# Four edits to the plan of a fused HGRN2 and multiplicative-FFN kernel on one Trainium2 core

## The chip, the core and the metric

The kernel runs on one core of one Trainium2 chip. The metric is device time in microseconds (us), the median of several executions. A profile of one further execution shows every instruction of the engines: TensorE (PE, with its weight loads as PEld), VectorE (DVE), ScalarE (ACT), GpSimd (POOL) and SyncE (SP), which issues the DMAs.

## What is computed

Two stages follow each other. The first is a gated linear recurrence for 4 batches of 8 heads, 768 steps and head size 48; the second is a feed-forward block on the 3072 resulting rows of 384.

```python
f = 1.0 / (1.0 + np.exp(-f_logit))
for t in range(S):
    state = f[:, :, t, :, None] * state + np.einsum('bhd,bhe->bhde', k[:, :, t], v[:, :, t])
    y[:, :, t] = np.einsum('bhd,bhde->bhe', q[:, :, t], state)
x = y.transpose(0, 2, 1, 3).reshape(B * S, H * D)
out = ((x @ w1) * (x @ w2)) @ w3 @ w_out
```

The sizes are w1, w2: 384 x 1024, w3: 1024 x 1024, w_out: 1024 x 384. The kernel multiplies w3 by w_out once (the "fold") and uses the 1024 x 384 product as the down weights.

## The kernel before

**The recurrence** is cut into 24 chunks (u = 0 to 23) of 128 steps, six per batch. A chunk's front runs on ACT and DVE: the gates (L526), a scan forward over them (fwd, L534), a reciprocal (L544), a scan backward (bwd, L556), and the products K = k * bwd (L564) and Q = q * fwd (L550). TensorE then takes chunks in *visits*. The visit of chunk u (L663, L589, L682, L695) computes the values of u, the pairs K Q of chunk u+1, what the state adds to the values of u, and the state's update from u+1. It needs K and Q of chunk u+1, K turned (kt) of u+1, the state at the middle of u (L791, with S from L794), and the masked pairs A of u, which GpSimd masks with two selects (L718). The state is then multiplied by a gain G (L841): in `state` (L847), on ACT from chunk 2 on (L851, four instructions).

**Turning K** has two ways. `turning` (L750) lets TensorE transpose K (four matmuls, L603) and ACT copy the result out of PSUM (L759) for chunks up to 6. From chunk 7 on it calls `crossing` (L730): ACT splits K into 16-bit halves (L735), a DMA transposes them (L738, "halves"), ACT merges them again (L743).

**From y to x.** ACT copies the values to `ys` (L878), two DMAs write them to DRAM (`yt`, L899) and one reads them back as a part of x^T (`xt`, L902).

**The feed-forward part** takes blocks of four chunks, 512 rows. Block 0 is done with plain products (L931, part names f<-xt,w); blocks 1 and 2 with a Strassen-like scheme of seven products (`seven`, L1027), which needs sums of x^T (L1001); blocks 3 to 5 with a scheme of fewer products and more sums (`many`, L1182). Each block's *down* product comes in two halves, `down(0)` and `down(1)`, each with seven products m1 to m7 (L931). They need four sums of the activations, S0 to S3 (`sum_`, L1286; the instruction is L1297, on VectorE): S0 and S1 for m5 and m6, S2 for m7, S3 for m3. DVE then adds the results up: u2 (L1310), u3 (L1323), c22 (L1334), c21 (L1340), c12 (L1348).

**What sets the order.** Nothing runs in the order in which the code is written. Every step is a task in `plan` with an engine, an estimated cost, what it depends on and a priority; `Plan.listed` (L187) fills a list by them and the instructions are written in that list's order. Each engine takes its own instructions strictly in this order, so a step whose input is late holds up all that stands behind it. `SURE_Z` (L82) is a time that the planner adds to the writing of `yt` before it lets x^T be read; it moves no instruction by itself, but what needs x^T is planned later. Where the plan before 130 us finds a gap on TensorE, `idle` (L403) fills it with matmuls that nothing uses (L407), one for each 0.43 us.

Of the kernel before, what the change touches and what calls it, by code (L numbers as in the profile page):

```python
# [40 lines left out]
ALU = mybir.AluOpType  # L41
# [3 lines left out]
B, H, S, D = 4, 8, 768, 48  # L45
# [11 lines left out]
UB = TB // C  # L57
# [3 lines left out]
NPE = 2  # L61
SOLO = 4
# [16 lines left out]
SURE_X = 1.0  # L79
SURE_W = 2.0  # L80
SURE_K = 1.0
SURE_Z = 0.8  # L82
NEED = (0.0, 1.0, 2.0, 3.0)
DUE = (5.0, 8.0, 24.0, 26.0)
EARLY = "23ACBD"
# [207 lines left out]
def rows(par):  # L293
    return slice(64 * par, 64 * par + D)
# [3 lines left out]
def ranged(ctx, tc, q, k, f_logit, v, w1, w2, w3, w_out, out, ident, w12, wc, left):  # L298

    nc = tc.nc  # L300
# [55 lines left out]
    abs_ = [at(10240 + KH * P * i, KH, P) for i in range(4)]  # L356
# [16 lines left out]
    plan = Plan()  # L373
# [37 lines left out]
    def heads(t):  # L411
        return t.rearrange("p (h c) -> p h c", c=C)
# [49 lines left out]
    def need(u):  # L462
        return NEED[u] if u < 4 else 60 + 14.5 * (u - 4)
# [286 lines left out]
    def turning(u):  # L750

        s, t = st[u], tk[u]
        if u > 6:
            crossing(u)
            return

        def turned():
            s["kt"] = work.tile([P, HP, R], F32, name="kt")
            nc.scalar.copy(s["kt"].rearrange("p (b two) r -> p b (two r)", two=2), s["pk"])  # L759

        if u < NPE:
# [38 lines left out]
    def rest(u):  # L800
        s, t = st[u], tk[u]
        opens, closes = u % NCH == 0, u % NCH == NCH - 1
        n0 = need(u)
# [34 lines left out]
        if not closes:  # L838
            def gains():
                s["G"] = work.tile([R, HP], F32, name="G")  # L840
                nc.gpsimd.tensor_tensor(s["G"], lasts[:, u], heads(gate[(u + 1) % 2][:, 0:NQ])[:, :, 0], ALU.mult)  # L841

            t["G"] = plan.add(
                "POOL", 0.3, gains, [t["l"]] + [tk[u + 1][nm] for nm in "g" if nm in tk[u + 1]] + past(u, 2, "d"), n0,
            )

            def state():  # L847
                gain = s["G"].unsqueeze(2).to_broadcast([R, HP, D])
                if u >= NPE:
                    for hp in range(HP):  # L850
                        nc.scalar.activation(s["S"][:, hp], s["S"][:, hp], AF.Copy, scale=s["G"][:, hp : hp + 1])  # L851
                    return
                s["S"] = work.tile([R, HP, D], F32, name="S")
                if opens:
                    nc.vector.tensor_tensor(s["S"], s["pd"], gain, ALU.mult)
                else:
                    nc.vector.tensor_tensor(s["S"], s["pd"], st[u - 1]["S"], ALU.add)
                    nc.vector.tensor_tensor(s["S"], s["S"], gain, ALU.mult)

            t["d"] = plan.add(  # L860
                *(("DVE", 0.36 if opens else 0.72) if u < NPE else ("ACT", 0.95)), state,
                [t["s"], t["G"]] + (past(u, 2, "b") if u < NPE else [t["mid"]]), n0, shared=u < NPE,
            )
# [22 lines left out]
        n = u // UB  # L886
# [28 lines left out]
        if u < NPE:  # L915
            t["z"] = plan.add("PE", 1.6, moved, [t["y"]], n0 - 996, takes=["f"], frees=[moving])
            t["x"] = plan.add("ACT", 0.55, settled, [t["z"]] + before, n0 - 20, frees=[t["z"]])
        else:
            t["z"] = moves(2, 197, 300, written, [t["y"]], n0 - 100, SURE_Z)
            t["x"] = moves(1, 197, 250, gathered, [t["z"]] + before, n0 - 100, SURE_X)  # L920


# [13 lines left out]
    def ffn(n):  # L936
        s = blk[n]
# [329 lines left out]
        def down(i):  # L1267
            q = {}
# [17 lines left out]
            def sum_(j):  # L1286
                def emit():
                    a11, a21 = quarter_(0, 0), quarter_(1, 0)
                    if j == 0:
                        x, y, op = a21, quarter_(1, 1), ALU.add  # L1290
                    elif j == 1:
                        x, y, op = abs_[0], a11, ALU.subtract
                    elif j == 2:
                        x, y, op = a11, a21, ALU.subtract
                    else:
                        x, y, op = quarter_(0, 1), abs_[1], ALU.subtract
                    nc.vector.tensor_tensor(abs_[j], x, y, op)  # L1297
                return emit

            def m1():  # L1300
# [55 lines left out]
            n0 = 100 * n + 90 + i + 60 * (n > 1) + 30 * (n == NB - 2)  # L1356
# [4 lines left out]
            def dve(nm, cost, emit, deps, pr=-200, **kw):  # L1361
                q[nm] = plan.add("DVE", cost, emit, deps, n0 + pr, **kw)

            def old(*names):
                return [downq[-2][nm] for nm in names] if len(downq) > 1 else []

            got0, got1 = (s["done"][i] + wc_sums for i in range(2))
            got = got0 + got1
            dve("S0", 0.69, sum_(0), got + old("m5"), -30)
            dve("S1", 0.69, sum_(1), [q["S0"]] + old("m6", "S3"), -30)  # L1370
            dve("S2", 0.69, sum_(2), got0 + old("m7"), -30)
            dve("S3", 0.69, sum_(3), [q["S1"]] + old("m3"), -30)
            pe("m1", m1, got + old("m7"), takes=["f"])
            q["k1"] = plan.add("ACT", 0.33, k1, [q["m1"]] + old("c21"), -200)
            pe("m6", m6, [q["m1"], q["S1"]], -3 if n == NB - 1 else -1, takes=["f"])
# [19 lines left out]
        for i in range(UB // 2):  # L1395
            q = down(i)
# [256 lines left out]
    for item in EARLY:  # L1653
# [4 lines left out]
        else:  # L1658
            t = tk[int(item)]
# [390 lines left out]
```

## Time and profile before

| | us |
|---|---|
| median of 3 runs | 456.38 (456.17 to 456.42) |
| the profiled execution's own time | 457.75 |
| its span, from the first to the last instruction | 456.0 |
| TensorE busy within the span | 445.6 |
| VectorE busy | 357.5 |
| ScalarE busy | 249.1 |
| GpSimd busy | 67.2 |

The profiled execution took 457.75 us, 1.75 us more than its span and 1.37 us more than the median. The granted TensorE clock was 1.0 throughout. In a timeline's row stand the start, the duration, the engine, the line, the operation, out<-in by tile, the shape, the count of instructions that were merged and, in brackets, the idle time ahead of it and what ended that. The trace counts each 32-bit matmul twice (x8 is four matmuls of the program). Consecutive matmuls overlap, so what a group costs TensorE is read from its start to the start of the next group.

### The profile page before, as it was taken

How to read it: one execution, taken by the hardware profiler on the slowest of the kernel's cores; microseconds unless marked ns; L12 is line 12 of the kernel's file. 1: busy time of each engine (PE TensorE's matmuls, PEld its weight loads, DVE VectorE, ACT ScalarE, POOL GpSimd, SP SyncE). 2: the span in 40 equal slices, each digit the busy share in tenths (PEclk: the TensorE clock that was granted, in tenths of full speed). 3: DMA queues.
4: the chain of work that ended last, by engine and by line, in shares of the span. 5: the costliest groups of instructions: out<-in, count | busy, mean ns of one | idle time of the engine just before them, and what ended most of it. 6: DMA issues, size and time to landing. Idle time of an engine off the chain costs nothing.

```text
span 456.0 us, 11696 instructions
## 1 busy us (share of the span) xinstructions
PE 445.6 (98%) x4732; PEld 388.5 (85%) x4732; DVE 357.5 (78%) x615; ACT 249.1 (55%) x557; POOL 67.2 (15%) x90
## 2 busy tenths in 40 slices
PE   7989999999999999999999999999999999999996
PEld 6778886666799888789998889998899988889995
DVE  8986999999999986999778949975669466766641
ACT  4564535535346665876665628665674656665000
POOL 9350000131221213231322110000000000000000
PEclk9999999999999999999999999999999999999999
DMA  6998899765338688899644057653364513330011
GB/s 184 271 298 249 269 339 290 239 200 108 96 101 203 172 181 166 197 177 199 162 129 89 21 169 235 200 189 114 96 194 161 201 47 92 93 92 3 35 70 39
DMA packets 59086, 72.65 MB, mean 159 GB/s; under 512 B 20994, under 2 KB 44163, under 8 KB 58003
## 3 DMA queue, kind: packets, MB, share of 16 engines
q1 hardware_dynamic: 59026, 71.85, 56.6%
q8 instruction: 38, 0.62, 0.6%
q14 instruction: 22, 0.17, 0.1%
HBM read 58.88 MB, written 9.04 MB: 149 GB/s over the span
## 4 chain that ended last, share of the span: by engine, by line
PE 88%; DVE 4%; POOL 3%; DMA 1%; ACT 1%; issue 1%; SPq 1%; DVEq 0%; POOLq 0%
PE f L931 25%; PE f L1027 13%; PE f L1182 11%; PE l L1182 11%; PE f L1499 9%; PE l L931 8%; PE py L663 3%; PE pa L589 2%; PE py L682 2%; PE pa L695 1%; POOL ab L445 1%; DMA xt<-yt 1%; DVE fwd L534 1%; POOL A L718 1%; DVE K L564 1%
## 5 line engine op out<-in xcount | busy, mean ns | idle before, releaser
L718 POOL TENSOR_SCALAR_AFFINE_SELECT A<-A 64x512 f32<-64x512 f32 (+1 forms) x46 | 45.6, 992 | 115.1 <-ACT A L712 111.2
L1499 PE MATMUL f<-place 128*128 128x384 f32 x128 | 42.8, 489 | 0.0
L931 PE MATMUL f<-xt,w 128*128 128x256 f32 x192 | 42.1, 380 | 0.0
L1027 PE MATMUL f<-xt,w 128*128 128x256 f32 x160 | 40.8, 380 | 0.0
L931 PEld LDWEIGHTS f<-xt,w 128*128 128x128 f32 x192 | 36.4, 190 | 4.9
L1499 PEld LDWEIGHTS f<-place 128*128 128x128 f32 x128 | 23.9, 190 | 15.3
L931 PE MATMUL f<-place 128*128 128x192 f32 x200 | 36.6, 329 | 0.1
L1027 PEld LDWEIGHTS f<-xt,w 128*128 128x128 f32 x160 | 30.4, 190 | 4.0
L931 PEld LDWEIGHTS f<-place 128*128 128x128 f32 x200 | 32.9, 190 | 0.9 <-PE f L931 0.3
L534 DVE TENSOR_TENSOR_SCAN fwd<-gate,floor 112x512 f32<-112x512 f32 x24 | 30.5, 1273 | 2.7 <-ACT lasts L539 1.1
L556 DVE TENSOR_TENSOR_SCAN bwd<-gate,back 112x512 f32<-112x512 f32 x24 | 29.8, 1240 | 0.8
L743 ACT COPY kt<-halves 128x896 uint16<-128x896 uint16 x17 | 20.4, 1199 | 16.4 <-DMA halves<-A 16.4
L1027 PE MATMUL f<-place 128*128 128x256 f32 x96 | 25.5, 388 | 0.0
L1435 ACT ACTIVATE place<-place 128x512 f32<-128x512 uint32 (+2 forms) x24 | 21.3, 889 | 6.0 <-DMA place<-in_w_dram 3.6
L851 ACT ACTIVATE S<-S,G 112x48 f32<-112x48 f32 x72 | 18.2, 327 | 10.9 <-DVE S L794 10.3
L526 ACT ACTIVATE gate<-f 112x512 f32<-112x512 f32 x22 | 13.9, 631 | 18.6 <-DMA f<-in_f_logit_dram 11.2
L841 POOL TENSOR_TENSOR G<-lasts,gate 112x4 f32<-112x4 f32 x20 | 10.9, 545 | 81.0 <-ACT lasts L539 28.9
L663 PEld LDWEIGHTS py<-A,vt 64*48 64x48 f32 (+1 forms) x672 | 13.6, 127 | 8.3 <-issue 6.3
L931 PE MATMUL f<-wc,ab 128*128 128x192 f32 x112 | 20.5, 326 | 0.0
L550 DVE TENSOR_TENSOR Q<-q,fwd 112x512 f32<-112x512 f32 x23 | 16.0, 694 | 4.8 <-PE py L682 4.8
L1027 PEld LDWEIGHTS f<-place 128*128 128x128 f32 x96 | 17.5, 190 | 2.4 <-ACT a L1068 0.2
L663 PE MATMUL py<-A,vt 64*48 64x64 f32 (+1 forms) x672 | 18.4, 223 | 0.7 <-POOL A L718 0.5
(281 smaller groups left out, 1051.7 us busy)
## 6 DMA issues: line engine op xcount, KB each, us to landing
place<-in_w_dram SPq DMA_DIRECT2D x21, 512.0 KB, 6.0
A<-in_w_dram SPq DMA_DIRECT2D x19, 512.0 KB, 4.2
place<-in_w_dram SPq DMA_DIRECT2D x8, 1024.0 KB, 5.7
q<-in_q_dram SPq DMA_DIRECT2D x46, 96.0 KB, 3.0
vt<-in_v_dram SPq DMA_DIRECT2D x23, 192.0 KB, 3.4
out_dram<-o SPq DMA_DIRECT2D x23, 192.0 KB, 2.1
k<-in_k_dram SPq DMA_DIRECT2D x44, 96.0 KB, 2.9
yt<-ys SPq DMA_DIRECT2D x44, 96.0 KB, 2.8
```

What stands on the lines that cost most here:

```text
L534: nc.vector.tensor_tensor_scan(s["P"], gate[u % 2][:, 0:NQ], floor, 0.0, ALU.mult, ALU.max)
L550: nc.vector.tensor_tensor(s["Q"], qu, s["P"], ALU.mult)
L556: nc.vector.tensor_tensor_scan(s["R"][:, ::-1], gate[u % 2][:, NQ:0:-1], back[:, ::-1], 0.0, ALU.mult, ALU.max)
L663: done = nc.tensor.matmul(y_block(u, hp, par, half)[p0 : p0 + w], lhsT=s["v"][half * W : half * W + W, h * D : h * D + w], rhs=s["A"][half ...
L718: nc.gpsimd.affine_select(out=a, in_=a, pattern=pattern, compare_op=ALU.is_ge, fill=0.0, base=0, channel_multiplier=-1,)
L743: nc.scalar.copy(to, halves.rearrange("p (two n) -> p two n", two=2))
L851: nc.scalar.activation(s["S"][:, hp], s["S"][:, hp], AF.Copy, scale=s["G"][:, hp : hp + 1])
L931: nc.tensor.matmul(out_, lhsT=lhs[i], rhs=rhs[i], start=start and i == 0, stop=i == len(lhs) - 1, skip_group_check=True,)
L1027: nc.tensor.matmul(q[nm][:, which * TH : which * TH + TH], lhsT=lhs[i](which), rhs=rhs[i], start=start and which == 0 and i == 0, stop=i = ...
L1182: nc.tensor.matmul(banks[g, c][:, which * TH : which * TH + TH], lhsT=lhs, rhs=x_node(a), start=first and which == 0, stop=True, skip_grou ...
L1435: nc.scalar.activation(part_.bitcast(F32), part_, AF.Copy, bias=2.0, scale=2.0**-51)
L1499: nc.tensor.matmul(w3s["p", jc], lhsT=w3s[jc][:, kc * P : kc * P + P], rhs=wos[:, kc], start=(kc == 0), stop=(kc == KF - 1),)
```

## The change

Four edits, all within tasks of the plan:

1. The sums S0 to S3 of blocks 0 and 1 (16 instructions of 128 x 512) go from VectorE to GpSimd, with a planned cost of 1.25 us in place of 0.69.
2. The gain on the state of chunks 2, 3 and 4 goes from ScalarE (four instructions a chunk) to VectorE (one a chunk).
3. The time added to the writing of `yt` was 0.8 us for every chunk from 2 on; it is now 0 up to chunk 8 and 2.5 us from chunk 9 on.
4. K of chunks 7 to 10 is turned on TensorE; the crossbar starts with chunk 11.

```diff
-SURE_Z = 0.8
+SURE_Z = 2.5
...
     def turning(u):
...
-        if u > 6:
+        if u > 10:
             crossing(u)
             return
...
             def state():
                 gain = s["G"].unsqueeze(2).to_broadcast([R, HP, D])
-                if u >= NPE:
+                if u > SOLO:
                     for hp in range(HP):
                         nc.scalar.activation(s["S"][:, hp], s["S"][:, hp], AF.Copy, scale=s["G"][:, hp : hp + 1])
+                    return
+                if u >= NPE:
+                    nc.vector.tensor_tensor(s["S"], s["S"], gain, ALU.mult)
                     return
...
-            t["z"] = moves(2, 197, 300, written, [t["y"]], n0 - 100, SURE_Z)
+            t["z"] = moves(2, 197, 300, written, [t["y"]], n0 - 100, SURE_Z if u > UB * 2 else 0.0)
...
-                    nc.vector.tensor_tensor(abs_[j], x, y, op)
+                    (nc.gpsimd if n < 2 else nc.vector).tensor_tensor(abs_[j], x, y, op)
...
+            def add_s(nm, emit, deps, pr):
+                q[nm] = plan.add("POOL" if n < 2 else "DVE", 1.25 if n < 2 else 0.69, emit, deps, n0 + pr)
...
-            dve("S0", 0.69, sum_(0), got + old("m5"), -30)
+            add_s("S0", sum_(0), got + old("m5"), -30)
```

S1 to S3 change as S0 does. NPE is 2, SOLO is 4, UB is 4.

**What it moves on GpSimd.** The selects of chunk 7 (the first two rows of "A<-A ... x2" here), 8, 9 and 10 and the gains between them stood in this order before; A is the masked pairs, G the gain:

```order
L718 AFFINE_SELECT A<-A 64x512 x2
L841 TENSOR_TENSOR G<-lasts,gate_95 112x4
L718 AFFINE_SELECT A<-A 64x512 x2
L841 TENSOR_TENSOR G<-lasts,gate_96 112x4
L718 AFFINE_SELECT A<-A 64x512 x4
```

Now the sums of block 0 (L1300, "place" and "ab" tiles) stand between them, from the selects of chunk 7 on:

```order
L718 AFFINE_SELECT A<-A 64x512 x2
L1300 TENSOR_TENSOR place<-ab 128x512 x2
L1300 TENSOR_TENSOR place<-place,ab 128x512
L1300 TENSOR_TENSOR place<-ab,place 128x512
L841 TENSOR_TENSOR G<-lasts,gate_95 112x4
L718 AFFINE_SELECT A<-A 64x512 x2
L841 TENSOR_TENSOR G<-lasts,gate_96 112x4
L1300 TENSOR_TENSOR place<-ab 128x512
L1300 TENSOR_TENSOR place<-place,ab 128x512
L718 AFFINE_SELECT A<-A 64x512 x2
L1300 TENSOR_TENSOR place<-ab 128x512
L1300 TENSOR_TENSOR place<-ab,place 128x512
```

Four sums stand ahead of the selects of chunk 8 and two ahead of those of chunk 9; the last two of block 0 follow.

**What it moves on VectorE.** At the end of block 0's products, before (ab<-f,ab is the last product of block 0, place<-ab are sums, A<-pa,S and S<-pa,A the state at the middle and the end of chunk 7, Q that of chunk 8, the f_1314 row u2):

```order
L1297 TENSOR_TENSOR place<-ab 128x512
L973 TENSOR_TENSOR ab<-f_1289,ab 128x256
L1297 TENSOR_TENSOR place<-ab 128x512
L1297 TENSOR_TENSOR place<-place,ab 128x512
L1297 TENSOR_TENSOR place<-ab,place 128x512
L791 TENSOR_TENSOR A<-pa,S 112x192
L794 TENSOR_TENSOR S<-pa,A 112x192
L550 TENSOR_TENSOR Q<-q_99,fwd 112x512
L1310 TENSOR_TENSOR place<-f_1314,place 128x192
```

Now, from the same product on (fwd, bwd, K and Q of chunk 9, fwd of chunk 10, the state of chunk 8, bwd of chunk 10, u2, K of chunk 10):

```order
L976 TENSOR_TENSOR ab<-f_1285,ab 128x256
L534 SCALAR_TENSOR_TENSOR fwd<-gate_96,floor 112x512
L544 RECIPROCAL back<-fwd 112x4
L556 SCALAR_TENSOR_TENSOR bwd<-gate_96,back 112x512
L564 TENSOR_TENSOR K<-k_101,bwd 112x512
L550 TENSOR_TENSOR Q<-q_97,fwd 112x512
L534 SCALAR_TENSOR_TENSOR fwd<-gate_95,floor 112x512
L791 TENSOR_TENSOR A<-pa,S 112x192
L794 TENSOR_TENSOR S<-pa,A 112x192
L544 RECIPROCAL back<-fwd 112x4
L556 SCALAR_TENSOR_TENSOR bwd<-gate_95,back 112x512
L1313 TENSOR_TENSOR place<-f_1424,place 128x192
```

The sums are gone from VectorE and the fronts of chunks 9 and 10 have come up to their place.

**What it moves on TensorE.** Behind the visit of chunk 6 stood three groups of block 0's up products, three fillers and then four products of `down(0)` (wc,ab is m1 and m2, place m6 and m7) ahead of the visit of chunk 7:

```order
L931 MATMUL f_1289<-xt,w_59 128x256 x3
L407 MATMUL f_1300<-floor 128x256 x3
L931 MATMUL f_1304<-wc,ab 128x192 x4
L931 MATMUL f_1314<-place 128x192 x4
L931 MATMUL f_1304<-wc,ab 128x192 x4
L931 MATMUL f_1314<-place 128x192 x4
```

Now a fourth group of up products, chunk 8's turn (ident,K), one filler and m1 stand there:

```order
L934 MATMUL f_1276<-xt,w_59 128x256 x3
L934 MATMUL f_1285<-xt,w_59 128x256 x3
L603 MATMUL f_1299<-ident,K 128x112 x4
L407 MATMUL f_1314<-floor 128x256
L934 MATMUL f_1316<-wc,ab 128x192 x4
```

The visit of chunk 7 follows, and behind it m2, chunk 9's turn, m6 and m5, then the visit of chunk 8:

```order
L695 MATMUL pa<-vt,kt 48x48 x16
L934 MATMUL f_1316<-wc,ab 128x192 x4
L603 MATMUL f_1414<-ident,K 128x112 x4
L934 MATMUL f_1424<-place 128x192 x4
L934 MATMUL f_1446<-place 128x192 x4
```

Three products of `down(0)` have gone behind the visit of chunk 7, and its m7 stands behind the visit of chunk 8 and chunk 10's turn, with m1 and m6 of `down(1)` between it and m4. One filler stands there where three stood; two stand where one stood behind the update of chunk 3. From chunk 7 on the visits come closer together, with less of the feed-forward work between them.

More of the change, by code (lines that the diff above doesn't have):

```diff
@@ L860, in rest @@
             t["d"] = plan.add(
-                *(("DVE", 0.36 if opens else 0.72) if u < NPE else ("ACT", 0.95)), state,
-                [t["s"], t["G"]] + (past(u, 2, "b") if u < NPE else [t["mid"]]), n0, shared=u < NPE,
+                *(("DVE", 0.36 if opens or u >= NPE else 0.72) if u <= SOLO else ("ACT", 0.95)), state,
+                [t["s"], t["G"]] + (past(u, 2, "b") if u < NPE else [t["mid"]]), n0, shared=u <= SOLO,
             )
@@ L1365, in old @@
                 return [downq[-2][nm] for nm in names] if len(downq) > 1 else []
+            def add_s(nm, emit, deps, pr):
+                q[nm] = plan.add("POOL" if n < 2 else "DVE", 1.25 if n < 2 else 0.69, emit, deps, n0 + pr)
             got0, got1 = (s["done"][i] + wc_sums for i in range(2))
             got = got0 + got1
-            dve("S0", 0.69, sum_(0), got + old("m5"), -30)
-            dve("S1", 0.69, sum_(1), [q["S0"]] + old("m6", "S3"), -30)
-            dve("S2", 0.69, sum_(2), got0 + old("m7"), -30)
-            dve("S3", 0.69, sum_(3), [q["S1"]] + old("m3"), -30)
+            add_s("S0", sum_(0), got + old("m5"), -30)
+            add_s("S1", sum_(1), [q["S0"]] + old("m6", "S3"), -30)
+            add_s("S2", sum_(2), got0 + old("m7"), -30)
+            add_s("S3", sum_(3), [q["S1"]] + old("m3"), -30)
             pe("m1", m1, got + old("m7"), takes=["f"])
```

## The prediction

> **What bounds the kernel now.** I read the page's busy times and its chain first.
>
> ```profile
> PE 445.6 (98%) x4732; PEld 388.5 (85%) x4732; DVE 357.5 (78%) x615; ACT 249.1 (55%) x557; POOL 67.2 (15%) x90
> PE 88%; DVE 4%; POOL 3%; DMA 1%; ACT 1%; issue 1%; SPq 1%; DVEq 0%; POOLq 0%
> ```
>
> TensorE is busy for 445.6 of 456.0 us and makes 88% of the chain. So an edit counts by what it adds to TensorE's own work, what it takes from it, and where TensorE has to wait; time freed elsewhere is worth nothing by itself. Next I read TensorE's timeline for its fillers, its turns of K, and its waits, each beside an undisturbed place of the same kind.
>
> ```profile
> 27.68 0.98 PE L663 MATMUL py<-A,vt 64*64 64x64 f32 x30 [0.55 <-POOL A L718]
> ...
> 70.36 5.32 PE L1499 MATMUL f<-place 128*128 128x384 f32 x16
> 75.52 0.55 PE L603 MATMUL f<-ident,K 112*128 112x112 f32 x4
> 75.91 5.34 PE L1499 MATMUL f<-place 128*128 128x384 f32 x16
> 81.18 0.70 PE L589 MATMUL pa<-Q,K 48*64 48x64 f32 x32
> ...
> 123.95 1.46 PE L407 MATMUL f<-floor 112*128 112x256 f32 x6
> 125.25 1.47 PE L931 MATMUL f<-wc,ab 128*128 128x192 f32 x8
> ...
> 158.69 0.45 PE L663 MATMUL py<-A,vt 64*64 64x64 f32 x16
> 158.96 0.64 PE L589 MATMUL pa<-Q,K 48*64 48x64 f32 x32
> ...
> 159.88 0.41 PE L682 MATMUL py<-Q,A 48*48 48x64 f32 x16
> 160.10 0.54 PE L695 MATMUL pa<-vt,kt 64*48 64x48 f32 x16
> 160.57 0.70 PE L1027 MATMUL f<-place,w 128*128 128x256 f32 x2
> ...
> 167.14 0.41 PE L682 MATMUL py<-Q,A 48*48 48x64 f32 x16
> 168.04 0.58 PE L695 MATMUL pa<-vt,kt 64*48 64x48 f32 x32 [0.50 <-ACT kt L743]
> ...
> 182.77 0.45 PE L663 MATMUL py<-A,vt 64*64 64x64 f32 x16
> 184.02 0.69 PE L589 MATMUL pa<-Q,K 48*64 48x64 f32 x32 [0.80 <-DVE S L794]
> ...
> 191.20 0.49 PE L663 MATMUL py<-A,vt 64*64 64x64 f32 x16
> 191.77 0.69 PE L589 MATMUL pa<-Q,K 48*64 48x64 f32 x32
> ```
>
> In the visit at 158.69 the second group starts 0.27 us after the first, and the whole visit takes 1.88 (158.69 to 160.57). At 182.77 the same step takes 1.25 and at 191.20 it takes 0.57: waits of 0.98 and 0.30. From the third group to the fourth it is 0.22 at 159.88 and 0.90 at 167.14: a wait of 0.68 for a K that came by the crossbar. These three, 1.96 us, are what I can still take away behind the fillers; 0.55 lies at the front, at 27.68.
>
> **The change part by part.** *Turning four chunks on TensorE.* The four transposes at 75.52 keep TensorE for 0.39 us, and the fold behind them takes 5.27 (75.91 to 81.18) where the one ahead took 5.16: another 0.11 for changing over. Three of the new turns stand among products, so 0.50 each; chunk 10's directly follows a visit, where the changeover is paid anyway, so 0.39. Together 1.89 us, all on the path, since TensorE has nothing to hide it behind. Before, a crossbar cost TensorE nothing and ACT and SP something; what these save is worth nothing while neither is waited for in chunks 7 to 10.
>
> *Fillers.* Three took 1.30 us (123.95 to 125.25), so 0.43 each. Two go there, one is added near 31 us: minus 0.43. That the gap they filled is truly gone is part of the shared-port term below.
>
> *The reads of x^T planned later.* Before, VectorE stood ready for block 2's sums and waited:
>
> ```profile
> 182.09 0.42 DVE L1001 TENSOR_TENSOR place<-xt 128x256 f32<-128x256 f32 x1 [2.44 <-DMA xt<-yt]
> ...
> 183.61 0.36 DVE L794 TENSOR_TENSOR S<-pa,A 112x192 f32<-112x192 f32 x1
> ```
>
> Behind that wait of 2.44 us on VectorE's queue stood the state and the next chunk's front, and S of 183.61 is what TensorE waited for at 184.02. The wait at 191.77 is the same delay, one chunk on. With the reads planned 1.7 us later, and in the new order four visits between chunk 11's and block 2's sums, both go: minus 1.28 us. If the read is later still, a wait of the same kind comes back with the next front behind it.
>
> *The gain of chunks 2 to 4 on VectorE.* It is one more short instruction a chunk there (no longer than the 0.36 of S) and lies beside TensorE's products, so nothing; at most the front's 0.55 goes or comes, since the new instruction stands between the state and a weight join, next to the selects that TensorE waits for at 27.68.
>
> *The sums on GpSimd.* This term decides. These rows show what VectorE and GpSimd do to each other; the POOL and DVE timelines first, then the groups by shape.
>
> ```profile
> 11.91 1.09 POOL L718 TENSOR_SCALAR_AFFINE_SELECT A<-A 128x1024 f32<-128x1024 f32 x1
> 46.93 0.20 POOL L841 TENSOR_TENSOR G<-lasts,gate 112x4 f32<-112x4 f32 x1 [12.28 <-issue]
> 95.99 1.71 POOL L718 TENSOR_SCALAR_AFFINE_SELECT A<-A 64x512 f32<-64x512 f32 x2 [1.08 <-ACT A L712]
> 117.32 1.09 POOL L841 TENSOR_TENSOR G<-lasts,gate 112x4 f32<-112x4 f32 x1 [6.59 <-ACT lasts L539]
> 134.71 1.37 POOL L718 TENSOR_SCALAR_AFFINE_SELECT A<-A 64x512 f32<-64x512 f32 x2 [3.21 <-ACT A L712]
> ...
> 86.11 0.69 DVE L564 TENSOR_TENSOR K<-k,bwd 112x512 f32<-112x512 f32 x1
> 96.03 1.15 DVE L564 TENSOR_TENSOR K<-k,bwd 112x512 f32<-112x512 f32 x1
> 117.19 1.23 DVE L556 TENSOR_TENSOR_SCAN bwd<-gate,back 112x512 f32<-112x512 f32 x1
> ...
> L534 DVE TENSOR_TENSOR_SCAN fwd<-gate,floor 112x512 f32<-112x512 f32 x24 | 30.5, 1273 | 2.7 <-ACT lasts L539 1.1 <-ACT gate L526 0.3
> L556 DVE TENSOR_TENSOR_SCAN bwd<-gate,back 112x512 f32<-112x512 f32 x24 | 29.8, 1240 | 0.8
> L1297 DVE TENSOR_TENSOR place<-ab 128x512 f32<-128x512 f32 x24 | 16.5, 687 | 0.2
> L973 DVE TENSOR_TENSOR ab<-f,ab 128x256 f32<-128x256 f32 x16 | 6.6, 420 | 4.3 <-PE f L931 4.2
> ```
>
> The gain G takes 0.20 us alone (46.93) and 1.09 where it starts just behind a scan (117.32): it ends with the scan, 117.19 + 1.23. K takes 0.69 alone and 1.15 where it starts with a select. So an instruction of VectorE with two operands in SBUF and one of GpSimd take turns, whole instruction by whole instruction; fwd, bwd, K and Q are all of that kind. A sum moved to GpSimd leaves VectorE's list but not this queue. The Trainium skill, page "SBUF — State Buffer", section "SBUF: two separate sides", says the same: VectorE and GpSimd share a port pair as an exclusive lock, held for the whole instruction, and that speaks against edit 1. The trace agrees, with the 1.09 and 1.15.
>
> How long a sum holds the queue no row shows. From below: half of the pair at 134.71, 0.69, less the 0.20 that an instruction of four elements takes, gives 0.49. From above: the select at 11.91 reads 1024 elements a partition, as many as a sum's two inputs, 1.09 less 0.20 gives 0.89. The Trainium skill, page "GPSIMD Engine Reference", section "3. Performance versus the Vector engine", has 4497 ns for a two-input add of 2048 elements; a quarter of it, as an estimate, is 1.12 us, and with that in place of 0.89 the term below would be about 1 us more. No run here shows it.
>
> Now the count, from the end of block 0's last up products on, in the new order. A product of the down part and one of the blocks behind it cost, from the chain:
>
> ```profile
> 410.87 0.86 PE f L1182 x4
> 447.69 1.30 PE f L931 x8
> ```
>
> So m1 and its like cost 1.30, a product of `seven`, two records of the same shape, 0.43. TensorE has a turn and a filler (0.82), m1, the visit, m2, a turn, m6 and m5 (four products 5.20, 1.88, 0.39) before the visit of chunk 8: 8.29 us. The queue has the last product (0.42), fwd 1.27, bwd 1.24, K and Q of chunk 9 (1.38), three sums at 0.89 (2.67) and chunk 8's selects (1.37): 8.35, or 9.62 if fwd of chunk 10 comes first. Up to chunk 10's turn TensorE has 10.17; the queue adds bwd and K of chunk 10 (1.93) and a sum of `down(1)`: 11.55 to 12.44. Up to m4, which needs u3, written behind bwd of chunk 11, TensorE has 14.46; the queue adds Q, a sum, fwd and bwd (4.09): 16.53, or 17.90 with the selects of chunk 9. So TensorE is held up by 2.1 to 3.4 us; with 0.49 for a sum, five sums take 2.0 us less and it is 0.1 to 1.4. What VectorE reads from PSUM in between runs beside GpSimd and can hide a sum. The term is 0 to 3.4; I take 1.7, the middle. For block 1 the same sums stand among visits that are 6 to 9 us apart by TensorE's work, with VectorE further ahead; I take nothing for them.
>
> **The sum**, against the profiled span: 456.0 + 1.89 - 0.43 - 1.28 + 1.7 = 457.9. With the 1.75 us around the span that is 459.6 for such an execution; the median of the runs was 1.37 below the profiled one, so 456.38 + 1.88 = 458.3 us. The wait of 0.68 stays in it, as chunk 12 still comes by the crossbar. About 0.2% (0.9 us) is what a measurement of this kernel can tell from no change.
>
> **The rivals.** *Faster:* the sums hide, their term is 0, and the 0.68 and 0.55 go too: 1.89 - 0.43 - 1.28 - 0.68 - 0.55 = -1.05, 455.3 us. For it speaks that VectorE loses 16 x 0.69 us of listed work where it is nearly full; it decides if a sum holds the queue for no more than the lower bound. Against it, both of those waits hang on other things than the sums. Chance 0.16.
>
> *No change:* the sums hide, but the 0.68 and 0.55 stay: +0.18, 456.6 us. The turns then just pay for the x^T wait. Chance 0.22.
>
> *The crossbar becomes the bound.* The visits of chunks 11 on come closer; the merges came 6.3 and 7.3 us apart at the fastest:
>
> ```profile
> 189.91 1.20 ACT L743 COPY kt<-halves 128x896 uint16<-128x896 uint16 x1 [0.97 <-DMA halves<-A]
> 196.25 1.22 ACT L743 COPY kt<-halves 128x896 uint16<-128x896 uint16 x1
> 203.58 1.20 ACT L743 COPY kt<-halves 128x896 uint16<-128x896 uint16 x1 [0.98 <-DMA halves<-A]
> ```
>
> Between the visits of chunks 11 to 17 TensorE has 14, 10, 12, 12, 14 and 10 products of `seven` at 0.43 and a visit of 1.88: 7.9, 6.2, 7.0, 7.0, 7.9 and 6.2 us. If every turn needs 7.3, the short ones lack 2.8 us, on top of the forecast 461.1. The slower merge of 7.3 did not hold TensorE up, which speaks against it. Chance 0.12.
>
> *The change does not do what it says:* the x^T read is late at its new place too, and 1.28 stays: 459.5 us. Chance 0.10.
>
> **How the numbers follow.** The forecast has the remaining 0.40; its own range is its port term's, 456.6 to 460.0. The range from 455.3 to 461.0 leaves out about half of the first rival's spread and half of the third's. Slower by over 0.2% are nearly all of the forecast and the last two rivals, 0.60; within 0.2% the second with the lowest edge of the forecast, 0.24; faster 0.16.
>
> **What would show it.** In the profile after: turns at four more places at 0.4 to 0.5 us each; sums on GpSimd of about 1.1 us, longer where a scan runs; scans and K lengthened beside them; new waits of TensorE between the visits of chunks 7 and 10, for selects (L718), K or u3, of 1 to 3 us in all; no wait for xt in front of block 2's sums. The forecast is wrong if TensorE runs through from chunk 7 to chunk 10 without waits, or if its largest waits lie behind chunk 11.

## The result, and the profile after

The changed kernel took 461.55 us (median; 459.69 to 462.83) beside 456.40 for the kernel before on the same chip: a ratio of 1.0100, 95% interval 1.0073 to 1.0128. So it is slower, as forecast, but by about 4.6 us and not by 1.9: 461.55 lies 0.55 above the upper end of the range, 461.0, and by the ratio from 456.38 it would be 460.9, just inside. The profiled execution took 461.57 us with a span of 459.8, 3.8 more than the 457.75 and 456.0 of before; the medians lie 5.15 apart, and the interval, 3.3 to 5.8 us, holds both differences.

The page of the changed kernel, its busy times and its chain by engine:

```profile
PE 447.0 (97%) x4746; PEld 389.1 (85%) x4746; DVE 359.2 (78%) x602; ACT 243.1 (53%) x541; POOL 99.4 (22%) x106
PE 85%; DVE 8%; issue 2%; DMA 2%; SPq 2%; POOL 1%; ACT 1%; DVEq 0%; POOLq 0%
```

TensorE's share of the chain falls from 88 to 85%, VectorE's rises from 4 to 8%. VectorE lost 16 sums of 0.69 us, 11 us, and is busy for 1.7 us longer than before: the three gains that edit 2 gave it take 1.8 (0.74, 0.35 and 0.67), and its other instructions have grown by about as much as the sums that left it, 10.9 us. TensorE's timeline shows where it now waits:

```profile
133.82 0.38 PE L663 MATMUL py<-A,vt 64*64 64x64 f32 x11 [0.38 <-POOL A L718]
...
137.26 0.60 PE L603 MATMUL f<-ident,K 112*128 112x112 f32 x4 [1.50 <-DVE K L564]
137.70 1.48 PE L934 MATMUL f<-place 128*128 128x192 f32 x8
...
142.31 1.57 PE L934 MATMUL f<-place,ab 128*128 128x192 f32 x8 [0.52 <-DVE place L1326]
...
150.59 1.54 PE L934 MATMUL f<-place 128*128 128x192 f32 x8 [0.73 <-DVE place L1313]
...
185.12 0.69 PE L589 MATMUL pa<-Q,K 48*64 48x64 f32 x32 [0.24 <-DVE S L794]
...
191.42 1.99 PE L1030 MATMUL f<-xt,place 128*128 128x256 f32 x8 [0.92 <-ACT place L1071]
```

The brackets give the idle time of the records; what TensorE loses from start to start is a little more (0.59 beside the 0.38 of the selects). Below, "lost" is the time from each matmul's start to the next one's, less the usual time for that shape, summed over a stretch (pieces of 0.15 us and more). Between 117 and 152 us the kernel before lost 0.2 us and the changed one 4.1 (selects 0.59, K 1.69, u3 0.69, u2 0.90, a filler's end 0.22); between 152 and 205 it was 2.0 and is 1.5; at the front, before 31 us, it is 0.6 less than it was. The four new turns take 0.44, 0.41, 0.39 and 0.44 from start to start (137.26 to 137.70 is the last), 1.7 us; one filler less gives 0.43 back. That is +3.9 - 0.5 - 0.6 + 1.7 - 0.4 = 4.1 for a span 3.8 us longer. No large wait stands behind 200 us.

What delays VectorE is seen where the first four sums stand, in GpSimd's and then VectorE's timeline of the changed kernel:

```profile
122.16 1.30 POOL L1300 TENSOR_TENSOR place<-ab 128x512 f32<-128x512 f32 x1
125.02 2.15 POOL L1300 TENSOR_TENSOR place<-ab 128x512 f32<-128x512 f32 x1 [1.57 <-DVE ab L976]
127.25 2.09 POOL L1300 TENSOR_TENSOR place<-place,ab 128x512 f32<-128x512 f32 x1
129.41 1.62 POOL L1300 TENSOR_TENSOR place<-ab,place 128x512 f32<-128x512 f32 x1
130.99 0.65 POOL L841 TENSOR_TENSOR G<-lasts,gate 112x4 f32<-112x4 f32 x1
131.59 2.18 POOL L718 TENSOR_SCALAR_AFFINE_SELECT A<-A 64x512 f32<-64x512 f32 x2
```

```profile
126.33 1.93 DVE L556 TENSOR_TENSOR_SCAN bwd<-gate,back 112x512 f32<-112x512 f32 x1
128.29 1.60 DVE L564 TENSOR_TENSOR K<-k,bwd 112x512 f32<-112x512 f32 x1
129.81 1.77 DVE L550 TENSOR_TENSOR Q<-q,fwd 112x512 f32<-112x512 f32 x1
131.68 1.63 DVE L534 TENSOR_TENSOR_SCAN fwd<-gate,floor 112x512 f32<-112x512 f32 x1
...
135.46 1.75 DVE L564 TENSOR_TENSOR K<-k,bwd 112x512 f32<-112x512 f32 x1
```

A sum took 1.30 us where nothing stood in its way. Read the rows as one queue: bwd ends at 128.26, the sum of 127.25 at 129.34, K at 129.89, the next sum at 131.03. So a sum holds the queue for 1.08 and 1.14 us, where I had 0.49 to 0.89, and bwd, K, Q and fwd take 6.93 us in place of 1.24 + 0.69 + 0.69 + 1.27 = 3.89. The selects of chunk 8, which stand behind four sums and a gain in GpSimd's own order, start at 131.59, and TensorE waits for them at 133.82; the K of 135.46 ends at 137.21, and TensorE turns it at 137.26. The Trainium skill, page "GPSIMD Engine Reference", section "3. Performance versus the Vector engine", has 4497 ns for an add of 2048 elements, and a quarter of it, 1.12 us, is the estimate that the prediction gave beside its own. The trace agrees with that, with 1.08 and 1.14, though partly by luck: the page's figure is the length of an instruction, and the sum's own record is 1.30.

The wait at 191.42 comes another way. GpSimd's timeline, then ScalarE's:

```profile
186.27 2.29 POOL L1300 TENSOR_TENSOR place<-ab 128x512 f32<-128x512 f32 x1 [4.04 <-DVE back L544]
188.53 0.65 POOL L841 TENSOR_TENSOR G<-lasts,gate 112x4 f32<-112x4 f32 x1
```

```profile
189.20 0.64 ACT L526 ACTIVATE gate<-f 112x512 f32<-112x512 f32 x1 [2.68 <-POOL G L841]
...
190.77 0.60 ACT L1071 COPY place<-f 128x512 f32<-128x512 f32 x1
```

The first sum of block 1 starts just behind bwd (186.25, 1.23 us) and takes 2.29; it ends 1.08 us after bwd, the same hold again. The gain G stands behind it on GpSimd, the next gate waits 2.68 us for G on ScalarE, and a copy of `seven` behind that gate is what TensorE waits for.

### The profile page after: what moved, and what is told of

Same layout as the page of the kernel before. It is cut to its first block, busy times and chain, and to the rows that moved or that the text cites. A ratio compares the mean times of both kernels' runs of the same rounds, so it can differ in the third digit from the quotient of the medians.

```text
span 459.8 us, 11718 instructions
## 1 busy us (share of the span) xinstructions
PE 447.0 (97%) x4746; PEld 389.1 (85%) x4746; DVE 359.2 (78%) x602; ACT 243.1 (53%) x541; POOL 99.4 (22%) x106
## 4 chain that ended last, share of the span: by engine, by line
PE 85%; DVE 8%; issue 2%; DMA 2%; SPq 2%; POOL 1%; ACT 1%; DVEq 0%; POOLq 0%
PE f L934 21%; PE f L1030 12%; PE f L1185 11%; PE l L1185 11%; PE f L1505 9%; PE l L934 8%; PE py L663 2%; PE l L1030 2%; PE pa L589 2%; DVE fwd L534 2%; PE py L682 2%; DVE K L564 1%; DVE bwd L556 1%; PE pa L695 1%; DVE Q L550 1%
## 5 line engine op out<-in xcount | busy, mean ns | idle before, releaser
L718 POOL TENSOR_SCALAR_AFFINE_SELECT A<-A 64x512 f32<-64x512 f32 (+1 forms) x46 | 50.2, 1092 | 85.3 <-ACT A L712 83.1
L934 PE MATMUL f<-xt,w 128*128 128x256 f32 x192 | 42.1, 380 | 0.0
L934 PEld LDWEIGHTS f<-xt,w 128*128 128x128 f32 x192 | 36.4, 190 | 4.9
L1505 PEld LDWEIGHTS f<-place 128*128 128x128 f32 x128 | 24.0, 190 | 15.4
L1030 PE MATMUL f<-xt,w 128*128 128x256 f32 x140 | 35.4, 380 | 0.0
L934 PEld LDWEIGHTS f<-place 128*128 128x128 f32 x184 | 30.2, 190 | 1.1 <-POOL A L718 1.0
L1030 PEld LDWEIGHTS f<-xt,w 128*128 128x128 f32 x140 | 26.5, 190 | 3.5
L934 PE MATMUL f<-wc,ab 128*128 128x192 f32 x144 | 26.8, 329 | 0.1
L934 PEld LDWEIGHTS f<-wc,ab 128*128 128x128 f32 x144 | 23.9, 190 | 0.9 <-PE f L407 0.5
L564 DVE TENSOR_TENSOR K<-k,bwd 112x512 f32<-112x512 f32 x22 | 21.9, 995 | 0.4
L881 ACT ACTIVATE ys<-py 112x512 f32<-112x512 f32 x22 | 13.0, 593 | 15.9 <-PE py L682 13.3
L663 PEld LDWEIGHTS py<-A,vt 64*64 64x64 f32 (+1 forms) x672 | 13.5, 127 | 7.8 <-issue 6.6
L663 PE MATMUL py<-A,vt 64*64 64x64 f32 (+1 forms) x672 | 18.4, 223 | 0.6 <-POOL A L718 0.4
```

The costliest lines, as they stand in the source:

```text
L564: nc.vector.tensor_tensor(s["K"], ku, s["R"], ALU.mult)
L663: done = nc.tensor.matmul(y_block(u, hp, par, half)[p0 : p0 + w], lhsT=s["v"][half * W : half * W + W, h * D : h * D + w], rhs=s["A"][half ...
L718: nc.gpsimd.affine_select(out=a, in_=a, pattern=pattern, compare_op=ALU.is_ge, fill=0.0, base=0, channel_multiplier=-1,)
L934: nc.tensor.matmul(out_, lhsT=lhs[i], rhs=rhs[i], start=start and i == 0, stop=i == len(lhs) - 1, skip_group_check=True,)
L1030: nc.tensor.matmul(q[nm][:, which * TH : which * TH + TH], lhsT=lhs[i](which), rhs=rhs[i], start=start and which == 0 and i == 0, stop=i = ...
L1505: nc.tensor.matmul(w3s["p", jc], lhsT=w3s[jc][:, kc * P : kc * P + P], rhs=wos[:, kc], start=(kc == 0), stop=(kc == KF - 1),)
```

## The experiments

All are ratios to the kernel before, with a 95% interval. Each ran beside the kernel before on its own chip; 0.001 is 0.46 us. Where "plan kept" is said, TensorE, ScalarE and SyncE have the same instructions in the same order as in the kernel named.

### Undoing edit 1, or edit 4

The first, sums_back, is the changed kernel with the sums on VectorE (n is the number of the block and never below 0); no_turns is the changed kernel without edit 4.

```diff
-                    (nc.gpsimd if n < 2 else nc.vector).tensor_tensor(abs_[j], x, y, op)
+                    (nc.gpsimd if n < 0 else nc.vector).tensor_tensor(abs_[j], x, y, op)
...
-                q[nm] = plan.add("POOL" if n < 2 else "DVE", 1.25 if n < 2 else 0.69, emit, deps, n0 + pr)
+                q[nm] = plan.add("POOL" if n < 0 else "DVE", 1.25 if n < 0 else 0.69, emit, deps, n0 + pr)
```

> The changed kernel with the sums of blocks 0 and 1 on VectorE again; the other three edits stay. Theory (the sums on GpSimd, through the queue that they share with fwd, bwd, K and Q, and through the gain G that stands behind them in GpSimd's own order, make five waits of TensorE between 117 and 150 us, 3.99 us, and the one of 1.08 at 190): those six go, 461.55 - 5.07 = about 456.5 us, 455.9 to 457.2. Rival 1 (the four turns bring the visits of chunks 8 to 10 closer together than VectorE can follow, whoever does the sums): VectorE then has even more to do, the waits between 117 and 150 stay, 459.5 us or more. Rival 2 (block 1 alone costs, by the order of GpSimd): not told apart here.

```diff
-        if u > 10:
+        if u > 6:
             crossing(u)
```

> The changed kernel with edit 4 undone: chunks 7 to 10 by the crossbar again, the sums of blocks 0 and 1 on GpSimd. Theory (the sums cost): most of the 5.07 us of waits stay or come back elsewhere; only the turns' 1.5 us go: 459 to 460.5 us. Rival 1 (the turns bring the visits too close): 457 us or less.

Measured: sums_back 1.0040 (1.0012 to 1.0067), no_turns 1.0136 (1.0105 to 1.0166). Without the sums on GpSimd the loss between 117 and 152 us is 0.2 us, with all four turns in place, so the rival that the turns bring the visits too close falls. But 1.8 us of slowing stay. And without the turns it does not get better by 1.5 us; the ratio is even 0.0036 higher, though the intervals overlap. Neither theory had that. The trace of no_turns, one execution, shows what came in, ScalarE first, then TensorE, then a table by stretch (its third number from the right is the granted clock):

```profile
157.13 1.19 ACT L743 COPY kt<-halves 128x896 uint16<-128x896 uint16 x1 [3.99 <-DMA halves<-A]
158.20 1.03 ACT L735 COPY A<-K 112x1024 uint16<-112x1024 uint16 x1
159.13 0.57 ACT L1071 COPY a<-f 128x512 f32<-128x512 f32 x1
```

```profile
153.61 1.89 PE L1030 MATMUL f<-place 128*128 128x256 f32 x8
159.76 1.22 PE L1030 MATMUL f<-place 128*128 128x256 f32 x2 [4.26 <-ACT a L1071]
```

```profile
155.00:159.70 4.70, 0.50 (x3) 0.09 (x1) 2.66 (x6) 2.56 (x4) 0.09 (x1) 0.79 0.97 270
159.70:163.40 3.70, 3.64 (x8) 2.52 (x8) 0.00 (x0) 2.06 (x8) 0.20 (x1) 0.50 0.91 187
```

The crossbar's merge waits 3.99 us for its transpose with the DMA engines busy for 97%, a copy of `seven` stands behind it, TensorE waits 4.26 us, and then runs for 3.7 us at half its clock. A crossbar that comes late is dear in this kernel, because of what ScalarE has behind it.

### Edit 1 alone, and edit 4 alone

The kernel before with the sums on GpSimd (the edit as above, the other way), and the kernel before with `u > 10`.

> The kernel before with edit 1 alone: the sums of blocks 0 and 1 on GpSimd, chunks 7 to 10 still by the crossbar. Theory (the sums cost by themselves): 456.4 plus 2 to 5 us, 458.5 to 461.5, with waits of TensorE for K, selects or u2 and u3 between 117 and 150 us. Rival 1 (only the turns together with the sums cost, since they bring the visits closer): 456 to 457, no new wait above 0.5 us between 117 and 150.

> The kernel before with edit 4 alone: chunks 7 to 10 turned on TensorE, the sums on VectorE. Theory: the four turns cost 1.6 to 1.9 us of TensorE and nothing else: 456.4 + 1.8 = 458.2, less up to 1 us if a filler or the crossbar's wait of 0.68 goes: 457.2 to 458.3. Rival 1 (the turns make VectorE late): waits of TensorE between 117 and 150 us of 2 us or more, 459.5 us or more.

Measured: only_sums 1.0143 (1.0117 to 1.0169), 6.5 us, above the range of both theories; only_turns 1.0026 (1.0006 to 1.0046), 1.2 us. The sums cost by themselves, without any turn, and by the medians more than in the full change, though the intervals overlap; the turns cost about what they take from TensorE, or a little less. In only_sums TensorE loses 3.6 us between 117 and 152, 3.0 between 152 and 205.

Another part of the profiled spans (462.8 and 458.2) is of neither edit. Up to 105 us PE, ACT, DVE and the DMA issues have in both kernels the order that they have in the kernel before, yet between 31 and 117 us TensorE loses 1.2 us more in only_sums and 1.9 more in only_turns, most of it ahead of chunk 5's turn at 88 us. There ScalarE's gate, at 74 to 77 us, waited 3.56 and 3.50 us for its part of f_logit to be read, where it had waited 2.37; the work behind it on ScalarE and VectorE came later, and with it K. So two single executions of the same instructions can differ by more than 1 us.

### The same plan, another engine

A new plan moves everything, so the engine of the sums was also changed with the plan kept: plan_kept_vector is the changed kernel whose 16 sums are issued by VectorE at the same places, and vplan_on_gpsimd is sums_back whose sums are issued by GpSimd.

```diff
-                    (nc.gpsimd if n < 2 else nc.vector).tensor_tensor(abs_[j], x, y, op)
+                    nc.vector.tensor_tensor(abs_[j], x, y, op)
```

> The changed kernel with its plan kept (TensorE, ScalarE and SyncE have the same instructions in the same order), only that the 16 sums of blocks 0 and 1 are issued by VectorE at the places where the plan has them. Theory (what costs is a sum's longer hold of the queue that both engines share, 1.30 us on GpSimd where VectorE needs 0.69, and GpSimd's own order behind it): the waits of 3.99 us between 117 and 150 shrink to less than half, the one of 1.08 at 190 goes: 2 to 4.5 us less than the changed kernel, 457 to 459.5 beside 456.4 of the kernel before. Rival (the order itself, with visits closer together, costs, whoever does the sums): no more than 1 us less, 460.5 or more.

> The plan of sums_back kept, in which the sums are VectorE's (TensorE, ScalarE and SyncE as there), but the 16 sums of blocks 0 and 1 are issued by GpSimd. Theory (a sum's longer hold and GpSimd's own order cost): 3 to 5 us more than sums_back, 461 to 463.5 beside 457.3 of the kernel before. Rival (the planner's other order is the cost, not the engine): within 1 us of sums_back, 457.5 to 459.5.

Measured: plan_kept_vector 1.0038 (1.0018 to 1.0057), vplan_on_gpsimd 1.0082 (1.0051 to 1.0112). With the changed kernel's plan the engine alone makes 0.0062, about 2.8 us (3.4 by the profiled spans, 459.8 and 456.4), and the intervals lie apart; with the other plan it makes 0.0042, about 1.9, with intervals that overlap. Where I expected 2 to 4.5 the first is in, and the second, 3 to 5 expected, is below. VectorE in plan_kept_vector, at the place shown above:

```profile
126.26 1.23 DVE L556 TENSOR_TENSOR_SCAN bwd<-gate,back 112x512 f32<-112x512 f32 x1
127.41 0.67 DVE L1300 TENSOR_TENSOR place<-place,ab 128x512 f32<-128x512 f32 x1
127.99 0.68 DVE L564 TENSOR_TENSOR K<-k,bwd 112x512 f32<-112x512 f32 x1
128.59 0.68 DVE L1300 TENSOR_TENSOR place<-ab,place 128x512 f32<-128x512 f32 x1
129.19 0.68 DVE L550 TENSOR_TENSOR Q<-q,fwd 112x512 f32<-112x512 f32 x1
129.98 1.48 DVE L534 TENSOR_TENSOR_SCAN fwd<-gate,floor 112x512 f32<-112x512 f32 x1
...
134.21 0.68 DVE L564 TENSOR_TENSOR K<-k,bwd 112x512 f32<-112x512 f32 x1
```

bwd starts at the same time in both (126.26 and 126.33); the K that chunk 10's turn waits for is done at 134.89 with VectorE doing all the work itself, and at 137.21 with GpSimd's help. TensorE loses 2.3 us between 117 and 152 in place of 4.1 (less than half was expected), and 0.5 in place of 1.5 behind it. Up to m4 it is 1.0 in place of 3.2 (0.22 for a filler's end, 0.60 for K, 0.20 for u3), so there the engine makes 2.2; the wait for u2 behind m4 is longer with VectorE, 1.31 against 0.90. The 2.3 us that are left stand in a plan laid out for a VectorE without the sums, and so are the order's; sums_back, planned with them, loses 0.2.

### One block's sums, and a truer cost

The condition `n < 2` becomes `n == 1` (sums_only_block1) or `n < 1` (sums_only_block0) in both places; true_cost has 2.0 for 1.25 in the plan.

> The changed kernel with the sums of block 1 alone on GpSimd, those of block 0 on VectorE. Theory (block 0's eight sums make the waits of 3.99 us between 117 and 150, block 1's first one the wait of 1.08 at 190 through the gain G behind it): 1 to 1.5 us over sums_back's 1.004, so 1.006 to 1.008 of the kernel before, a wait of TensorE for a copy of ScalarE behind G near the first sum of block 1. Rival (block 1's sums cost nothing, as predicted): 1.004, as sums_back. Rival 2 (block 1's make most of the cost): 1.009 or more.

> The changed kernel with the sums of block 0 alone on GpSimd, those of block 1 on VectorE. Theory (block 0's eight sums make the cost, 0.6% of the kernel's time, block 1's nothing, as sums_only_block1 with 1.0036 beside 1.004 says): 1.009 to 1.011 of the kernel before, waits of 3 us or more between 117 and 150. Rival (only all sixteen together cost): 1.006 or less.

> The changed kernel with the planner told 2.0 us for a sum on GpSimd instead of 1.25 (a sum took 1.3 to 2.3 in the trace). Theory (the sums stand where the planner believes the queue free and it isn't, but the queue is also full): the order moves, part of the waits goes, 0 to 2 us less than the changed kernel, 459.5 to 461.5. Rival 1 (only the wrong cost in the plan makes the loss): 3 us less or more, 458.5 or below. Rival 2 (the queue is simply too full): no less.

Measured: block 1 alone 1.0036 (1.0013 to 1.0059), no more than sums_back, so the theory's 1.006 to 1.008 failed and the rival, that they cost nothing, held; block 0 alone 1.0114 (1.0091 to 1.0138), above the range I gave; true_cost 1.0061 (1.0040 to 1.0082), 0.0039 or 1.8 us less than the changed kernel and so in the theory's 0 to 2, though the intervals overlap a little. Between 117 and 152 us TensorE loses 0.2 us with block 1's sums on GpSimd and 4.4 with block 0's. So block 0's sums, which stand where VectorE has the fronts of chunks 9 to 11 in a row, make the cost, and block 1's can be had for nothing in another order. The excess of sums_only_block0 has a source of its own. Near its end TensorE waits once more:

```profile
422.35 1.03 PE L1185 MATMUL l<-xt,K 128*128 128x256 f32 x4
424.90 1.57 PE L934 MATMUL f<-place 128*128 128x192 f32 x8 [1.53 <-DVE place L1313]
```

It loses 1.7 us there, 0.0037, which the changed kernel does not: a group of small instructions of VectorE that checks ranges (from L1589 on) came ahead of the sums that the last block needs. That is the plan's accident and nothing of block 0. With the truer cost the loss between 117 and 152 goes from 4.1 to 3.0 us, and the loss behind it from 1.5 to 0.2: the wrong price was a part of the loss, not all of it. The profiled span is only 0.8 us shorter (459.0), since the front loses 0.4 more and the end, from TensorE's last matmul on, takes 6.0 us in place of 4.7; there two of the range checks (L1624, L1625) stand ahead of the last sum of results.

### Each sum in two halves

Plan kept; each sum on GpSimd becomes two instructions of 256 elements a partition.

```diff
-                    (nc.gpsimd if n < 2 else nc.vector).tensor_tensor(abs_[j], x, y, op)
+                    if n < 2:
+                        for h in (slice(0, KH // 2), slice(KH // 2, KH)):
+                            nc.gpsimd.tensor_tensor(abs_[j][:, h], x[:, h], y[:, h], op)
+                        return
+                    nc.vector.tensor_tensor(abs_[j], x, y, op)
```

> The changed kernel, plan kept, each sum on GpSimd cut into two instructions of 256 elements a partition. Theory (VectorE waits out whole instructions of GpSimd, one by one): an instruction of VectorE then waits for half a sum, 0.65 instead of 1.3 us, so K, Q and the scans beside the sums are lengthened by less, and the waits of 3.99 us between 117 and 150 shrink by 1 us or more: 1.006 to 1.0085 of the kernel before. Rival (what counts is the time of all the sums together in the queue and in GpSimd's order): 1.0095 to 1.012, no less or a little more for twice the instructions.

Measured 1.0068 (1.0046 to 1.0091), 1.5 us below the changed kernel, in the theory's range; the intervals overlap, and the profiled spans say 1.4 (458.4 and 459.8). But it is not where I expected it. K next to the sums is shorter, as said; the two rows are the K of 128.29 and of 135.46 in the changed kernel:

```profile
128.29 1.05 DVE L564 TENSOR_TENSOR K<-k,bwd 112x512 f32<-112x512 f32 x1
...
134.68 0.82 DVE L564 TENSOR_TENSOR K<-k,bwd 112x512 f32<-112x512 f32 x1
135.43 3.46 DVE L550 TENSOR_TENSOR Q<-q,fwd 112x512 f32<-112x512 f32 x1
```

```profile
135.02 0.38 PE L663 MATMUL py<-A,vt 64*64 64x64 f32 x11 [1.20 <-POOL A L718]
```

K no longer holds TensorE up, but the two halves of a sum take 1.4 us where a whole one took 1.3, the selects come later, and TensorE waits for them twice, 0.44 and 1.20 us: between 117 and 152 it loses 3.6 us, against 4.1. The gain is behind it, 0.5 against 1.5: G starts at 186.29 and is done at 186.90, where it was done at 189.18, and the copy of `seven` is not late. That is not the half's length alone: the first half had run at 182.00 already, and the second started at 185.09, just ahead of the bwd of 185.14, where the whole sum came just behind bwd. So the hold by whole instructions is shown by K, and the sum of the work in the queue is the larger part of the loss.

### Edits 2 and 3 alone, and three more turns

z_gain is the kernel before with edits 2 and 3; sb_turn13 is sums_back with `u > 13` in `turning`.

> The kernel before with edits 2 and 3 alone (gain of chunks 2 to 4 on VectorE, reads of x^T planned later). Theory as predicted (the waits of 0.98 and 0.30 behind block 2's sums go, nothing else moves): 1.28 us less, 0.997 of the kernel before. Rival (the wait for x^T goes, but ScalarE, with the crossbar's merge ahead of the copies of seven, holds TensorE up by about as much a little later, as at 177 us in sums_back): 0.999 to 1.001, a wait of about 1 us for a copy of L1068 between 165 and 195 us. Rival 2 (these two edits cost by themselves): 1.0025 or more.

> sums_back (sums on VectorE, edits 2 to 4 kept) with chunks 11 to 13 turned on TensorE as well, the crossbar from chunk 14. Theory (the wait of 1.07 at 177 us in sums_back is for a copy that stands behind the crossbar's merge on ScalarE): that wait goes or comes later, three turns add 1.2 to 1.5 us: 1.0035 to 1.006 of the kernel before. Rival (the crossbar costs more than one such wait between chunks 11 and 13): 1.002 or less. Rival 2 (a turn costs more than 0.5 us, since the front must be ready earlier): 1.008 or more.

Measured: z_gain 1.0040 (1.0014 to 1.0066), the second rival's value and not the theory's 0.997; sb_turn13 1.0067 (1.0041 to 1.0093). In z_gain VectorE no longer waits for x^T ahead of block 2's sums. It waits ahead of block 1's, where the kernel before had no wait; VectorE, then TensorE, then the clock by stretch:

```profile
148.40 0.43 DVE L1004 TENSOR_TENSOR place<-xt 128x256 f32<-128x256 f32 x1 [2.24 <-DMA xt<-yt]
...
149.73 0.36 DVE L794 TENSOR_TENSOR S<-pa,A 112x192 f32<-112x192 f32 x1
```

```profile
150.14 0.69 PE L589 MATMUL pa<-Q,K 48*64 48x64 f32 x32 [1.61 <-DVE S L794]
...
152.66 2.98 PE L1030 MATMUL f<-place 128*128 128x256 f32 x8 [0.42 <-ACT a L1071]
```

```profile
152.60:155.40 2.80, 2.74 (x8) 2.30 (x9) 2.66 (x4) 1.94 (x7) 0.00 (x0) 0.62 0.51 132
```

It is the wait of before, one block earlier, with S behind it. Edit 3 has two halves: from chunk 9 on the planner adds 2.5 us, up to chunk 8 it adds nothing where it added 0.8, and block 1's sums read chunks 4 to 7. That the missing 0.8 us makes this wait fits the rows; edit 2 was not taken out of z_gain, and the changed kernel without edit 3 was not tried, so it is argued and not shown. In the changed kernel and in sums_back this wait is not there; their plans, with chunks 7 to 10 turned on TensorE, put block 1's sums elsewhere. In sums_back the loss of 1.07 us at 177 us is ScalarE's queue:

```profile
176.62 1.20 ACT L743 COPY kt<-halves 128x896 uint16<-128x896 uint16 x1 [1.43 <-DMA halves<-A]
177.68 0.58 ACT L1071 COPY a<-f 128x512 f32<-128x512 f32 x1
```

```profile
178.31 1.99 PE L1030 MATMUL f<-place 128*128 128x256 f32 x8 [0.91 <-ACT a L1071]
```

sb_turn13 bears this out: with chunks 11 to 13 turned on TensorE no piece of 0.15 us is lost between 152 and 205. Its time is a little above the theory's 1.0035 to 1.006, and it has the loss of 1.7 us of the range checks as well, ahead of 420.81; less that, 0.0037, it would be 1.003. No version that ran is faster than the kernel before.

## Why the prediction was right in direction and short in size

**The port term was right in kind, and mis-sized.** Sums on GpSimd wait out fwd, bwd, K and Q, and these wait out the sums; new waits for selects, K and u3 stand between the visits of chunks 7 and 10. The step that failed is the hold of a sum: "From above: the select at 11.91 reads 1024 elements a partition, as many as a sum's two inputs, 1.09 less 0.20 gives 0.89." A sum holds the queue for 1.08 to 1.14. The row was no bound, for a select and an add are different operations. With 1.10 for 0.89 the same count, five sums, gives 3.15 to 4.45 us up to m4 instead of 2.1 to 3.4; the trace has 3.2 there (0.22 + 0.59 + 1.69 + 0.69). Taking 1.7, the middle between two counts, was the second error: both ends of the hold came from other operations, and the nearer one was the upper. The estimate of 1.12 from the Trainium skill, page "GPSIMD Engine Reference", section "3. Performance versus the Vector engine", by which the term was about 1 us more, was the better price, partly by luck; the trace agrees with it, as shown above. With the plan kept and VectorE doing the sums, 1.0 of the 3.2 stays, so the count names the right queue and has a part of the order in it.

**"For block 1 ... I take nothing for them" is half right.** Block 1's sums alone cost nothing in their own plan (1.0036 beside 1.0040). In the changed kernel the first of them delays G, and with that 1.1 us at 190. I had asked what the sums do to VectorE's queue, and not what stands behind them on GpSimd.

**The turns:** 1.7 us from start to start, 1.9 forecast, and 1.2 us by only_turns. In company they seem to cost less than that: without them the ratio is 1.0136, with them 1.0100, with intervals that overlap. The trace of no_turns gives a reason, a crossbar transpose that lands late at a place where ScalarE cannot wait for it. That "a crossbar cost TensorE nothing" holds only while it lands in time.

**The reads of x^T:** "both go: minus 1.28 us" was wrong as a sum. The wait ahead of block 2's sums shrank to 1.29 us on VectorE (it starts at 178.05 in the changed kernel) and no longer reaches TensorE by itself; but 0.46 for S at 184.7 and 1.1 for the copy at 190 came in its place, and edits 2 and 3 alone cost 0.0040. I priced the half of the edit that adds 1.7 us and not the half that takes 0.8 away. The crossbar's 0.68, said to stay, went. The gains of edit 2, put at no more than 0.36 us each, took up to 0.74, and the front lost less all the same. With the front's 0.6 TensorE lost 1.1 us less in these places, beside the 1.28 forecast; that the two come near each other is luck.

**What would have shown it wrong** did not come: TensorE does not run through chunks 7 to 10, and its largest wait, 1.69, lies there. Of the rivals, "the sums hide" fell with 4.1 us lost between 117 and 152, and the crossbar as a bound between chunks 11 and 17 fell too: of the 1.5 us lost there, none was a wait for a K that came by the crossbar.

What stays open: by the runs, edits 2 to 4 together cost 1.8 us (sums_back), while sums_back's profiled execution, the fastest of its runs, has a span of 454.3, below the 456.0 of before. Its slower executions were not profiled, so what they lose is not known. Single executions of a kernel here spread by 1.4 to 6.6 us; inputs that are read late, as at 74 to 77 us in only_sums and only_turns, can make 1 to 2 us of such a difference, and the rest is open.

## What to carry to other kernels

Before an operation goes from VectorE to GpSimd, price its hold of the queue that both share by the same operation, not by another of the same size, and count it against VectorE where the two run at once: sixteen sums of 11 us taken off VectorE left it busy for 356.6 us in only_sums, where it had been 357.5. Ask also what stands behind it in GpSimd's own order, and who waits for that. Where a planner orders everything, test an engine with the plan kept as well; between plans, a wait that goes can come back at another place.

## What the runs showed of the hardware that was not expected

**No fair turns.** In the halved kernel the Q of 135.43 took 3.46 us. GpSimd's timeline there:

```profile
135.52 1.44 POOL L1302 TENSOR_TENSOR place<-ab 128x256 f32<-128x256 f32 x2
136.91 1.42 POOL L1302 TENSOR_TENSOR place<-place,ab 128x256 f32<-128x256 f32 x2
138.29 2.64 POOL L718 TENSOR_SCALAR_AFFINE_SELECT A<-A 64x512 f32<-64x512 f32 x2
```

Four instructions of GpSimd ran one after the other while Q stood waiting, and Q's 0.69 us came only then. In the changed kernel's rows at 126 to 133 us the two engines took turns one by one. The Trainium skill, page "SBUF — State Buffer", section "SBUF: two separate sides", says that whichever starts first has the pair for its whole instruction; that agrees, but it says nothing of who is next.

**Half a clock after a wait.** TensorE's granted clock fell to 0.50 after the wait of 4.26 us in no_turns. In vplan_on_gpsimd a wait of 2.35 was enough: the clock was 0.50 from 129.55 to 132.30, and eight records that take 1.46 us took 2.77:

```profile
128.00 1.75 PE L934 MATMUL f<-place 128*128 128x192 f32 x8 [2.35 <-POOL place L1300]
129.55 2.77 PE L934 MATMUL f<-wc,ab 128*128 128x192 f32 x8
```

In z_gain waits close together, 0.29 and 1.61 us and then 0.42, went with a stretch at 0.62. After 1.50 us in the changed kernel and 2.15 in only_sums it stayed at 1.0. So a wait of some 2 us can cost a microsecond or two more behind it, and which one does, these runs do not settle. The Trainium skill, page "TensorE: Matmul & The Clock Gate", section "What's actually happening", has the clock halved after an idle window of about 3.4 us that runs freely; the 4.26 agrees, and the 2.35 is shorter than that, so the measurement decides.
